# Moving a seven-for-eight block product from the second to the first product of each MLP layer

## The chip, the cores and the metric

The kernel runs on one core of one Trainium2 chip. The metric is device time in microseconds (us); one execution is also recorded by the hardware profiler, and all rows below come from that record. TensorE (PE) multiplies and loads its weights (PEld) from on-chip memory (SBUF) and writes only to its accumulators (PSUM, 8 banks of 512 fp32 values per partition). VectorE (DVE) and ScalarE (ACT) read and write both, GpSimd (POOL) works on SBUF, and SP issues the transfers between the chip's main memory and SBUF.

## The reference, cut to what matters

```python
X = np.fft.rfft(x, axis=1)                        # x: 2 x 3008 x 256
y = np.fft.irfft(X * (filt_r + 1j * filt_i), n=3008, axis=1).reshape(6016, 256)
g = y @ w_gate                                    # 256 -> 1536
y = (g / (1 + np.exp(-g)) * (y @ w_val)) @ w_out  # 1536 -> 256
h = y @ w_in                                      # 256 -> 2048
out = (h * np.clip(h + 3, 0, 6) / 6) @ w_out2     # 2048 -> 256
```

The two layers are called layer 1 and layer 2 below, and in each of them the first product goes from 256 to the wide side and the second product comes back.

## The kernel before

**Precision.** Both products must be better than one pass of TensorE gives. Each operand is split into a high part (a cast to the matmul type, on ACT) and a low part (the rest, a subtraction), and each product is made of three matmuls: low weight times high data, high weight times high data, high weight times low data. The helper `split` and the methods `high` and `low` are these splits.

**Stages.** First comes the Fourier stage (`over_n1`, `over_n2`, `filter_product`, `back`), which reads x and the filters and writes the spectrum to the buffers `d2` in main memory. `to_time` turns a part of it into one block of activations. A block has 512 tokens (448 for the last of each of the two batches), and there are 12 blocks. Then come layer 1 for all blocks and layer 2 for all blocks. Layer 1 writes its results to `yd`, layer 2 reads them back (`load_y`, `split_y`).

**The weights** arrive as 64-bit words. `Decode` makes fp32 of them in six steps (`part`, on DVE, the last one mostly on POOL). While layer 1 works on the first two blocks, which alternate, its weights are decoded one hidden chunk of 128 at a time and split into `wall`, where they stay until layer 1 ends. Layer 2's output weights are decoded during layer 1, put aside in `wd`, and brought back and split on ACT and POOL at the end of layer 1; its input weights are split into `wi2`.

**The two products.** One step takes a pair of hidden chunks and one block. `l1` is the plain first product: 12 matmuls of 512 columns per chunk in layer 1 (gate and value), 6 in layer 2. `l2` is the second product in the scheme of seven block products for eight (two chunks by two output halves by two token halves): 7 products of 3 matmuls are 21 matmuls of 256 columns. Its operands are sums: `Hidden.differences`, `rest`, `high` and `low` form the sums of the activations on DVE and split them, `weight_sums` forms those of the weights, and `gather` adds the seven products up at the end of a block. For the first two blocks of layer 1 the second product is plain (`l2_plain`, 12 matmuls of 512 columns per pair).

**What sets the order.** The program is written out by hand; each engine works through its instructions in that order and waits for semaphores. PSUM is divided into four banks `gv` for first products and four banks `a` for second products. In layer 1 the second product of a pair follows one pair later, in layer 2 two pairs later, so that its operands have a pair's time or more to be formed.

The excerpt below shows the lines that the change touches: `l1` is line 232, `l2` line 244, `l2_plain` line 254, `minus` and `plus` are lines 110 and 113 (all subtractions and additions on DVE and POOL are recorded under these two), `split` is line 117, the activation and product of layer 1 are lines 626 and 635, those of layer 2 lines 772 and 773.

Of the kernel before, what the change touches and what calls it, by code (L numbers as in the profile page):

```python
# [16 lines left out]
P = 128  # L17
# [29 lines left out]
def _token_times(time):  # L47

    order = []
    for j, n in BLOCKS:  # L50
# [28 lines left out]
def fft_conv_glu_mlp(ctx: ExitStack, tc: tile.TileContext, x, filt, mats, sgn, w1, w2, out):  # L79
# [44 lines left out]
    def new_g():  # L124
        return work.tile([P, 7 * D], F32, tag="g", name="g", bufs=1)

    def turns(j, n):

        return 32 * j // N1, -(-(32 * j + n // 2) // N1)

    def load_g(b, j):
        t0, t1 = turns(*BLOCKS[j][:1], BLOCKS[j][1] * N2)
        g = new_g().rearrange("p (t c) -> p t c", c=D)
        for r in range(2):
            nc.sync.dma_start(out=g[rows(r, N1P), :t1 - t0],
                              in_=d2[b].rearrange("q (h n) c -> (q h) n c", h=2)[:, 32 * r + t0:32 * r + t1])
        return g[:, :, :P], g[:, :, P:]

    def new_xs():
        return work.tile([P, 2, 2, 512], F32R, tag="xs", name="xs")  # L140

    def to_time(g, j, tag="gv"):

        accs = [bank(tag), bank(tag)]
        first, n = BLOCKS[j][0], BLOCKS[j][1] * N2
        t0, t1 = turns(first, n)
        lo, hi = 32 * first, 32 * first + n // 2
        for a in range(2):
            for t in range(t0, t1):
                i0, i1 = max(lo, t * N1), min(hi, (t + 1) * N1)  # L150
                for o in range(0, P, 64):
                    for r in range(2):
                        nc.tensor.matmul(accs[r][o:o + 64, a * 256 + i0 - lo:a * 256 + i1 - lo],  # L153
                                         g[a][rows(r, N1P), t - t0, o:o + 64],
                                         mat[rows(r, N1P), FIN + i0 - t * N1:FIN + i1 - t * N1])
        return accs

    def time_halves(xs, accs, j, r):
        n = BLOCKS[j][1] * 32
        src = accs[r].rearrange("p (a n) -> p a n", a=2)[:, :, :n]  # L160
        return xs[:, 0, :, r * n:(r + 1) * n], xs[:, 1, :, r * n:(r + 1) * n], src
# [55 lines left out]
    PAIRS = ((0, 0), (1, 2), (4, 5), (5, 4), (2, 6), (3, 3), (6, 1))  # L217
    PLACE = ((0, 0), (0, 1), (1, 0), (1, 1), (2, 0), (2, 1), (3, 0))
    WHERE = dict(zip(("P1", "P2", "P6", "P7", "P4", "P5", "P3"), PLACE))

    blocks = [(b, j) for b in range(B) for j in range(NB)]
    n_block = len(blocks)

    def ntok(k):
        return BLOCKS[blocks[k][1]][1] * N2

    def l1(acc, w, xs, n, part=(0, 1, 2)):

        for i in part:
            r, v = ((0, 0), (0, 1), (1, 0))[i]  # L230
            for k in range(2):
                nc.tensor.matmul(acc[:, :n], w[:, r, k * P:(k + 1) * P], xs[:, v, k, :n],  # L232
                                 start=(r, v, k) == (0, 0, 0), stop=(r, k) == (1, 1))

    def l2(acc, w, hidden, first, last):
        hs, nt = hidden.hs, hidden.nt

        terms = list(zip(PAIRS, PLACE))
        if last:
            terms.sort(key=lambda term: term[0][1] > 2)  # L240
        for v, ws in ((0, (1, 0)), (1, (0,))):
            for (iw, ih), (b, h) in terms:
                for r in ws:
                    nc.tensor.matmul(acc[b][:, 256 * h:256 * h + nt], w[:, r, iw], hs[:, v, ih, :nt],  # L244
                                     start=first and h == 0 and v == 0 and r == 1,
                                     stop=last and v == 1 and (h == 1 or b == 3))

    def l2_plain(acc, w, hidden, first, last):
        hs = hidden.hs
        for v, ws in ((0, (1, 0)), (1, (0,))):  # L250
            for j in range(2):
                for i in range(2):
                    for r in ws:
                        nc.tensor.matmul(acc[j], w[:, r, ((0, 1), (3, 2))[j][i]], hs[:, v, 2 * i:2 * i + 2],  # L254
                                         start=first and (v, i, r) == (0, 0, 1), stop=last and (v, i) == (1, 1))
# [8 lines left out]
    class Hidden:  # L264


        def __init__(self, nt):
            self.nt = nt
            self.h = mlp.tile([P, 8, 256], F32, tag="h", name="h")

        def chunk(self, i):
            return self.h[:, 2 * i:2 * i + 2, :self.nt]

        def halves(self, bank):
            return bank[:, :2 * self.nt].rearrange("p (t n) -> p t n", t=2)

        def values(self, a, b):
            return self.h[:, a:b, :self.nt]

        def parts(self, r, a, b):  # L280
            return self.hs[:, r, a:b, :self.nt]

        def begin(self, pool):

            self.differences(pool)
            self.rest()

        def differences(self, pool):

            self.hs = pool.tile([P, 2, 7, 256], F32R, tag="hs", name="hs", bufs=2 if pool is mlp else 1)  # L290
            v = self.values
            nc.scalar.copy(out=self.parts(0, 0, 3), in_=v(1, 4))  # L292
            minus(v(4, 6), v(1, 3), v(0, 1).to_broadcast([P, 2, self.nt]))

        def rest(self):

            v = self.values
            plus(v(6, 7), v(5, 6), v(1, 2))
            minus(v(7, 8), v(6, 7), v(3, 4))
            minus(self.parts(1, 0, 3), v(1, 4), self.parts(0, 0, 3).bitcast(F32))  # L300

        def high(self):
            nc.scalar.copy(out=self.parts(0, 3, 7), in_=self.values(4, 8))  # L303

        def low(self):
            minus(self.parts(1, 3, 7), self.values(4, 8), self.parts(0, 3, 7).bitcast(F32))

        def plain(self, pool):

            self.hs = pool.tile([P, 2, 7, 256], F32R, tag="hs", name="hs", bufs=2)  # L310
            split(self.parts(0, 0, 4), self.parts(1, 0, 4), self.values(0, 4))

    def new_y():
        return work.tile([P, 1024], F32, tag="y", name="y", bufs=1)

    def gather(acc, nt, scale, last=None):

        y = new_y()[:, :4 * nt]
        q = y.rearrange("p (j t n) -> p j t n", j=2, t=2)
        at = {name: acc[b][:, 256 * h:256 * h + nt] for name, (b, h) in WHERE.items()}  # L320

        def step(o, name, other):
            if scale == 1.0:
                plus(o, other, at[name])
            else:
                nc.vector.scalar_tensor_tensor(out=o, in0=at[name], scalar=scale, in1=other,
                                               op0=ALU.mult, op1=ALU.add)

        c00, c01, c10, c11 = q[:, 0, 1], q[:, 0, 0], q[:, 1, 1], q[:, 1, 0]
        nc.scalar.mul(out=c01, in_=at["P1"], mul=scale)  # L330
        p45 = work.tile([P, 2, 256], F32, tag="sm", name="p45", bufs=1)[:, :, :nt]
        nc.scalar.mul(out=p45, in_=acc[2].rearrange("p (h n) -> p h n", h=2)[:, :, :nt], mul=scale)
        step(c10, "P6", c01)
        step(c00, "P2", c01)
        step(c11, "P7", c10)
        step(c01, "P3", c10)
        minus(c10, c11, p45[:, 0])
        both = y.rearrange("p (j t) -> p j t", j=2)
        if last:
            for j, engine in ((1, nc.sync), (0, nc.scalar)):  # L340
                minus(q[:, j, 0], q[:, j, 0], p45[:, 1])
                engine.dma_start(out=last[j], in_=both[:, j])
            return
        minus(q[:, :, 0], q[:, :, 0], p45[:, 1:2].to_broadcast([P, 2, nt]))
        return both
# [497 lines left out]
```

## Time and profile before

| | us |
|---|---|
| median of 3 runs (1168.34 to 1170.76) | 1169.61 |
| the profiled execution, its own time | 1174.74 |
| its span, first to last instruction | 1172.9 |
| PE busy in the span | 1156.9 |
| DVE busy | 1009.5 |
| ACT busy | 610.6 |
| POOL busy | 145.5 |

The profiled execution took 5.13 us more than the median, and its span is 1.84 us shorter than its own time. The profile is read from the top down. The busy times say which engine is full; the 40 slices say whether it is full throughout; the waits of that engine say how long it stood and for whom; the chain of waits, which goes back from the last instruction, says which pieces of work follow one another without a gap. The Fourier stage ends at about 79 us, the alternating first two blocks at about 189 us, layer 1 at about 665 us.

### The profile page before, as it was taken

The numbers are of one execution on the slowest core, as the hardware profiler recorded it, in microseconds if no ns is written. First come the engines' busy times: TensorE is split into PE (matmuls) and PEld (weight loads), VectorE is DVE, ScalarE is ACT, GpSimd is POOL, SyncE is SP. The second block draws the span as 40 slices with busy tenths as digits, with TensorE's granted clock in tenths as the row PEclk, the third lists the DMA queues.
The fourth block names the chain that finished last, engine by engine and source line by source line (L and its number), as shares of the span: only waits on it lengthen the run. The fifth ranks groups of instructions, "written<-read, shape, count | busy, mean of one in ns | idle before, by whom it ended". The sixth has DMA issues, their size and how long they took to land.

```text
span 1172.9 us, 21793 instructions
## 1 busy us (share of the span) xinstructions
PE 1156.9 (99%) x9036; PEld 1024.6 (87%) x9036; DVE 1009.5 (86%) x1575; ACT 610.6 (52%) x928; POOL 145.5 (12%) x152
## 2 busy tenths in 40 slices
PE   9989999999999999999999999999999999999997
PEld 7668888888899888888889988999999999899997
DVE  5879967776678888778888899999999999999997
ACT  5555434343434444444445555656666566666654
POOL 4643210000002222012122300000000000000000
PEclk9999999999999999999999999999999999999999
DMA  8873401110013230312103111011001101100100
GB/s 297 271 194 106 142 14 44 25 36 18 22 57 86 84 109 24 98 46 72 53 3 106 57 35 36 1 37 36 30 6 37 34 1 37 37 21 17 35 18 18
DMA packets 43301, 70.33 MB, mean 60 GB/s; under 512 B 3712, under 2 KB 25088, under 8 KB 43200
## 3 DMA queue, kind: packets, MB, share of 16 engines
q1 hardware_dynamic: 42512, 68.17, 19.1%
q8 instruction: 71, 1.16, 0.4%
q10 hardware_dynamic: 688, 0.75, 0.2%
q14 instruction: 30, 0.25, 0.1%
HBM read 46.62 MB, written 22.28 MB: 59 GB/s over the span
## 4 chain that ended last, share of the span: by engine, by line
PE 91%; DVE 4%; DMA 2%; issue 1%; ACT 1%; SPq 1%; POOL 0%; ACTq 0%; DVEq 0%
PE gv L232 52%; PE a L244 31%; PE a L254 3%; DVE hs L110 1%; PE gv L463 1%; PE gv L153 1%; PE a L437 1%; DMA xin<-x_in 1%; PE gv L421 1%; DVE h L773 1%; DVE h L110 1%; SPq L472 1%; ACT h L772 0%; DMA d<-turned 0%; DVE h L113 0%
## 5 line engine op out<-in xcount | busy, mean ns | idle before, releaser
L244 PEld LDWEIGHTS a<-hs,wall 128*128 128x128 f32 x3276 | 408.7, 191 | 12.9 <-ACT hs L303 1.0
L244 PE MATMUL a<-hs,wall 128*128 128x256 f32 (+1 forms) x3276 | 414.6, 282 | 1.3 <-issue 0.5
L232 PE MATMUL gv<-xs,wall 128*128 128x512 f32 (+1 forms) x1728 | 398.9, 386 | 0.0
L232 PEld LDWEIGHTS gv<-xs,wall 128*128 128x128 f32 x1728 | 320.9, 188 | 58.7 <-issue 1.2
L110 DVE TENSOR_TENSOR hs<-h,hs 128x768 fp32r<-128x768 f32 (+2 forms) x324 | 348.0, 1074 | 6.3 <-ACT hs L117 3.4
L232 PE MATMUL gv<-xs,wi 128*128 128x512 f32 (+1 forms) x1152 | 274.5, 387 | 0.0
L232 PEld LDWEIGHTS gv<-xs,wi 128*128 128x128 f32 x1152 | 210.2, 188 | 35.7
L303 ACT CAST hs<-h 128x1024 fp32r<-128x1024 f32 (+1 forms) x156 | 160.8, 1031 | 128.0 <-DVE h L110 127.9
L110 DVE TENSOR_TENSOR h<-h 128x512 f32<-128x512 f32 (+3 forms) x312 | 186.4, 597 | 6.7
L292 ACT CAST hs<-h 128x768 fp32r<-128x768 f32 (+1 forms) x156 | 128.1, 821 | 101.5 <-DVE h L635 69.5
L635 DVE TENSOR_TENSOR h<-h,gv 128x512 f32<-128x512 f32 (+1 forms) x144 | 96.8, 672 | 71.9 <-PE gv L232 65.0
L626 ACT ACTIVATE h<-gv 128x512 f32<-128x512 f32 (+1 forms) x144 | 84.8, 589 | 136.1 <-PE gv L232 135.2
L773 DVE SCALAR_TENSOR_TENSOR h<-h,gv 128x512 f32<-128x512 f32 (+1 forms) x192 | 128.9, 671 | 14.2 <-ACT h L772 8.0
L772 ACT ACTIVATE h<-gv 128x512 f32<-128x512 f32 (+1 forms) x192 | 108.6, 589 | 59.0 <-PE gv L232 39.4
L113 DVE TENSOR_TENSOR h<-h 128x256 f32<-128x256 f32 (+1 forms) x156 | 65.7, 421 | 2.1
L113 POOL TENSOR_TENSOR ww<-ww,wa 128x512 f32<-128x512 f32 x16 | 20.7, 1296 | 371.2 <-issue 191.6
L254 PE MATMUL a<-hs,wall 128*128 128x512 f32 x144 | 34.6, 389 | 0.0
L254 PEld LDWEIGHTS a<-hs,wall 128*128 128x128 f32 x144 | 27.0, 188 | 5.6
L110 POOL TENSOR_TENSOR wall<-x,wall 128x512 fp32r<-128x512 f32 (+1 forms) x20 | 23.9, 1217 | 59.4 <-ACT wall L492 59.4
L463 PE MATMUL gv<-us,mat 64*64 64x384 f32 x256 | 29.6, 522 | 1.4 <-issue 0.9
L110 POOL TENSOR_TENSOR us<-us 128x192 f32<-128x192 f32 x32 | 25.9, 808 | 28.3 <-DVE us L450 27.4
L428 ACT COPY first<-gv 128x384 f32<-128x384 f32 x30 | 14.5, 482 | 28.2 <-PE gv L421 28.2
(79 smaller groups left out, 622.6 us busy)
## 6 DMA issues: line engine op xcount, KB each, us to landing
raw<-w_in SPq DMA_DIRECT2D x16, 512.0 KB, 4.4
xin<-x_in SPq DMA_DIRECT2D x30, 256.0 KB, 5.2
x<-w_in SPq DMA_DIRECT2D x9, 768.0 KB, 4.7
d<-turned SPq DMA_DIRECT2D x32, 192.0 KB, 5.0
yd<-y SPq DMA_DIRECT2D x10, 512.0 KB, 2.9
g<-yd SPq DMA_DIRECT2D x10, 512.0 KB, 3.7
y_out<-y SPq DMA_DIRECT2D x20, 256.0 KB, 2.4
wt<-wd SPq DMA_DIRECT2D x8, 448.0 KB, 3.2
```

The lines of the kernel that those rows point to most:

```text
L110: (engine or nc.vector).tensor_tensor(out=out, in0=a, in1=b, op=ALU.subtract)
L113: (engine or nc.vector).tensor_tensor(out=out, in0=a, in1=b, op=ALU.add)
L232: nc.tensor.matmul(acc[:, :n], w[:, r, k * P:(k + 1) * P], xs[:, v, k, :n], start=(r, v, k) == (0, 0, 0), stop=(r, k) == (1, 1))
L244: nc.tensor.matmul(acc[b][:, 256 * h:256 * h + nt], w[:, r, iw], hs[:, v, ih, :nt], start=first and h == 0 and v == 0 and r == 1, stop=las ...
L254: nc.tensor.matmul(acc[j], w[:, r, ((0, 1), (3, 2))[j][i]], hs[:, v, 2 * i:2 * i + 2], start=first and (v, i, r) == (0, 0, 1), stop=last a ...
L292: nc.scalar.copy(out=self.parts(0, 0, 3), in_=v(1, 4))
L303: nc.scalar.copy(out=self.parts(0, 3, 7), in_=self.values(4, 8))
L463: nc.tensor.matmul(accs[r][rows(h), :2 * COLS].rearrange("p (o n) -> p o n", o=2), mat[rows(r), w:w + N2], u[rows(r), :, part], start=m == ...
L626: nc.scalar.activation(out=h, in_=hid[p].halves(gate), func=AF.Silu)
L635: nc.vector.tensor_tensor(out=h, in0=h, in1=hid[p].halves(val), op=ALU.mult)
L772: nc.scalar.activation(out=h, in_=pre, func=AF.Relu, bias=3.0)
L773: nc.vector.scalar_tensor_tensor(out=h, in0=h, scalar=6.0, in1=pre, op0=ALU.min, op1=ALU.mult)
```

## The change

Blocks are now 1,024 tokens (960 for the last of each batch), six in all. The first block is still done as two blocks of 512 with plain products while layer 1's weights are decoded. From then on the work is a list of 108 **units**: 60 of layer 1 (five blocks by 12 chunks) and 48 of layer 2 (six blocks by 8 pairs of chunks).

- The first product of a unit is the scheme of seven products for eight (token halves by two halves of the 256 inputs by gate and value, or by the two chunks of a pair). Each of the seven, named `00`, `01`, `11`, `S1` to `S4` after its weights, is 3 matmuls over half a block (512 or 480 columns). Its sums are formed in PSUM: ACT copies bank b1 into bank b2, TensorE adds further products to both, and DVE adds b2 to an SBUF copy (`s7`), once into bank b3 and once into SBUF (`v1`).
- The second product is plain: 12 matmuls in layer 1 and 24 in layer 2, issued by `fill` in pieces between the seven products of the next unit.
- `Hidden`, `l2` and `gather` go. The sums of the activations are formed once per block instead (`differ`, `x_high`, `x_low`: 4 subtractions, 7 casts, 7 subtractions).
- Weights don't stay split. They are kept in main memory as fp32 together with their sums (`w1f`, `w2f`); each unit's weights are fetched (`ask_unit`) and split on ACT and POOL (`split_unit`), again for every block.
- Work beside the units (decoding layer 2's weights, forming their sums, preparing the next block) is placed at four **spots** in each unit, A, B, C and T. `turn_x`, at spot T of two units per block in layer 1, runs `to_time` into two of the four `gv` banks and empties them. `take` empties the banks `a` of a finished block in the first unit of the next one, half on DVE and half on ACT.

```diff
         def low_w1(f, engine=None):
...
+            nc.sync.dma_start(out=w1f[f][:, :6 * P], in_=w)
...
+        def split_unit(s, engine=nc.gpsimd):
...
+                split(form[:, 0], form[:, 1], src[:, wide:wide + 7 * P], engine)
+                split(wo[:, 0], wo[:, 1], src[:, :wide], engine)
...
+        def product(acc, s, a, i, start):
+            k = units[s][0]
+            n, w = half(k), wu[s][0]
+            for q, (r, v) in enumerate(((0, 0), (0, 1), (1, 0))):
+                nc.tensor.matmul(acc[:, :n], w[:, r, FORM[a] * P:(FORM[a] + 1) * P], xs_part(k, v, i),
+                                 start=start and q == 0, stop=q == 2, skip_group_check=True)
...
+        for g in range(G2):
             for i in range(2):
...
+                s = F1 * (1 + g // 2) + 3 * (g % 2) + i
+                add(s - 1, "C", ask_w2, g, i)
+                add(s, "A", lambda g, i: dec2[g, i].start(), g, i)
+                add(s, "B", lambda g, i: (dec2[g, i].part(0), dec2[g, i].part(1)), g, i)
+                add(s, "C", lambda g, i: dec2[g, i].part(2), g, i)
+                add(s + 1, "A", lambda g, i: (dec2[g, i].part(3), dec2[g, i].part(4)), g, i)
+                add(s + 1, "B", lambda g, i: dec2[g, i].part(5), g, i)
+                add(s + 1, "C", keep_w2, g, i)
...
+            product(b1, s, "00", 0, True)
+            if prev.kind:
+                prev.act(1, 0, pending[:, :prev.n])
+            product(b3, s, "S3", 5, True)
+            nc.scalar.copy(out=b2[:, :n], in_=b1[:, :n])
+            if prev.kind:
+                prev.times(1, 0, prev.v1 if prev.kind == 1 else pending[:, :prev.n])
+            fill()
+            nc.scalar.copy(out=u.s7, in_=b3[:, :n])
+            if prev.kind == 2:
+                prev.act(1, 1, prev.v1)
+                prev.times(1, 1, prev.v1)
+            if prev.kind:
+                prev.high(1)
+            spot(s, "A")
+            product(b2, s, "S2", 4, False)
+            plus(b3[:, :n], b2[:, :n], u.s7)
+            product(b1, s, "01", 1, False)
+            u.act(0, 0, b1[:, :n])
+            split_unit(s + 2)
+            if prev.kind:
+                prev.low(1)
+            fill()
+            if f == 0:
+                take(prev, 0)
+            spot(s, "B")
+            product(b2, s, "S1", 3, False)
+            if kind == 2:
+                u.times(0, 0, b1[:, :n])
+            plus(u.v1, b2[:, :n], u.s7)
+            product(b3, s, "11", 6, False)
+            if kind == 2:
+                u.act(0, 1, b3[:, :n])
+            u.times(0, kind - 1, b3[:, :n])
+            fill()
+            u.high(0)
+            free, role = pending, [b1, b3, b2]
+            spot(s, "T")
+            product(b2, s, "S4", 2, False)
+            spot(s, "C")
+            u.low(0)
+            fill()
```

On TensorE in the middle of layer 1 the order before alternates whole first products (`L232`: gate and value of one chunk into two `gv` banks, then those of the other chunk) with whole second products (`L244`, into four banks `a`).

```order
L232 MATMUL gv_3316<-xs_2963,wall_74 128x512 x6
L232 MATMUL gv_3317<-xs_2963,wall_74 128x512 x6
L232 MATMUL gv_3340<-xs_2963,wall_74 128x512 x6
L232 MATMUL gv_3341<-xs_2963,wall_74 128x512 x6
L244 MATMUL a_3288<-hs_3330,wall_74 128x256 x4
L244 MATMUL a_3289<-hs_3330,wall_74 128x256 x4
L244 MATMUL a_3290<-hs_3330,wall_74 128x256 x4
L244 MATMUL a_3291<-hs_3330,wall_74 128x256 x2
L244 MATMUL a_3288<-hs_3330,wall_74 128x256 x2
L244 MATMUL a_3289<-hs_3330,wall_74 128x256 x2
L244 MATMUL a_3290<-hs_3330,wall_74 128x256 x2
```

One unit of layer 1 after the change, with `L645` the seven products (into the banks gv0 to gv3, here b1 = gv2, b3 = gv3, b2 = gv0) and `L690` the pieces of the second product of the unit before:

```order
L645 MATMUL gv2_109<-xs_4372,wu_5355 128x512 x3
L645 MATMUL gv3_110<-xs_4372,wu_5355 128x512 x3
L690 MATMUL a0_111<-hs_5389,wo_5252 128x512 x2
L690 MATMUL a2_113<-hs_5389,wo_5252 128x512 x2
L645 MATMUL gv0_107<-xs_4372,wu_5355 128x512 x3
L645 MATMUL gv2_109<-xs_4372,wu_5355 128x512 x3
L690 MATMUL a0_111<-hs_5389,wo_5252 128x512
L690 MATMUL a2_113<-hs_5389,wo_5252 128x512
L690 MATMUL a1_112<-hs_5389,wo_5252 128x512 x2
L645 MATMUL gv0_107<-xs_4372,wu_5355 128x512 x3
L645 MATMUL gv3_110<-xs_4372,wu_5355 128x512 x3
```

All matmuls are now 512 columns wide (or 480), a unit's seven products return to the same three banks within the unit, and between two uses of bank gv0 stand 7 matmuls (the 3 of `01` or `11` and the 4 of `fill`).

On VectorE before, where a word of layer 2's weights is decoded (`ww`, `wa`) in layer 1: the product with the gate, the sums of the activations and their low parts follow.

```order
L193 TENSOR_SCALAR ww_3784<-wa_3757 128x512
L196 SCALAR_TENSOR_TENSOR ww_3784<-raw_3714,ww_3784 128x512
L199 TENSOR_SCALAR wa_3757<-ww_3784 128x512
L201 SCALAR_TENSOR_TENSOR wa_3757<-raw_3714,wa_3757 128x512
L635 TENSOR_TENSOR h_3759<-h_3759,gv_3794 128x2x224
L110 TENSOR_TENSOR h_3759<-h_3759 128x2x224
L113 TENSOR_TENSOR h_3759<-h_3759 128x224
```

One unit of layer 1 after, in which the same work stands at the spots (A: two rows ahead of the first addition `L119`, B: two rows ahead of the second, C: one row behind the product):

```order
L672 TENSOR_TENSOR h_4082<-h_4082 128x512
L200 TENSOR_SCALAR wa_4098<-ww_4119 128x512
L202 SCALAR_TENSOR_TENSOR wa_4098<-raw_4076,wa_4098 128x512
L119 TENSOR_TENSOR gv1_108<-gv2_109,h_4145 128x512
L116 TENSOR_TENSOR hs_4081<-h_4082,hs_4081 128x512
L192 TENSOR_SCALAR wa_4163<-wa_4163 128x512
L194 TENSOR_SCALAR ww_4185<-wa_4163 128x512
L119 TENSOR_TENSOR h_4145<-gv2_109,h_4145 128x512
L672 TENSOR_TENSOR h_4145<-h_4145,gv1_108 128x512
L197 SCALAR_TENSOR_TENSOR ww_4185<-raw_4139,ww_4185 128x512
L116 TENSOR_TENSOR hs_4144<-h_4145,hs_4144 128x512
```

The two additions `L119`, for which TensorE's next product into b2 waits, now stand behind the decoding steps of spots A and B in VectorE's row.

On POOL before, the last work is seven splits of a weight pair (`wt`) at the end of layer 1, and layer 2 has none:

```order
L110 TENSOR_TENSOR wi2_5177<-ww_6447,wi2_5177 128x2x256
L110 TENSOR_TENSOR wall_74<-wt_6774,wall_74 128x896
L110 TENSOR_TENSOR wall_74<-wt_6801,wall_74 128x896
L110 TENSOR_TENSOR wall_74<-wt_6874,wall_74 128x896
L110 TENSOR_TENSOR wall_74<-wt_6940,wall_74 128x896
L836 UNCONDITIONAL_BRANCH
```

After, POOL splits a unit's weights (`wu` and `wo` from the fetched `st`) in every unit to the end:

```order
L116 TENSOR_TENSOR wu_9659<-st_9555,wu_9659 128x896
L116 TENSOR_TENSOR wo_9660<-st_9555,wo_9660 128x512
L116 TENSOR_TENSOR wu_9729<-st_9627,wu_9729 128x896
L116 TENSOR_TENSOR wo_9730<-st_9627,wo_9730 128x512
L934 UNCONDITIONAL_BRANCH
```

There are 108 such pairs of rows (`wo` is 256 wide in the 60 units of layer 1).

## Rows read from the trace of the kernel before

**Rows 1.** The page: busy us, share and instructions; TensorE's granted clock in tenths.

```profile
PE 1156.9 (99%) x9036; PEld 1024.6 (87%) x9036; DVE 1009.5 (86%) x1575; ACT 610.6 (52%) x928; POOL 145.5 (12%) x152
...
PEclk9999999999999999999999999999999999999999
```

**Rows 2.** Waits of PE: for whom, us in total, times, longest.

```profile
PE gv L421 <- issue: 3.4, 3, 1.7
PE a L153 <- DMA g<-d: 2.3, 2, 1.8
```

**Rows 3.** Chain of waits, first two blocks: start us, us, what.

```profile
135.78 5.44 PE gv L232 x24
141.22 2.72 PE a L254 x12
```

**Rows 4.** The same chain, blocks of 512 in layer 1 and in layer 2.

```profile
317.04 2.51 PE a L244 x21
319.55 5.47 PE gv L232 x24
...
926.09 2.51 PE a L244 x21
928.61 2.75 PE gv L232 x12
```

**Rows 5.** The same chain, blocks of 448 in layer 1.

```profile
334.91 4.87 PE gv L232 x24
339.78 2.34 PE a L244 x21
```

**Rows 6.** The same chain, blocks of 448 in layer 2.

```profile
1147.50 2.43 PE gv L232 x12
1149.93 2.33 PE a L244 x21
```

**Rows 7.** Timeline, layer 2: start us, us, engine, operation, [idle before <-releaser].

```profile
1036.39 2.67 PE L244 MATMUL a<-hs,wall 128*128 128x256 f32 x21
1036.59 0.60 ACT L772 ACTIVATE h<-gv 128x512 f32<-128x512 f32 x1 [0.31 <-PE gv L232]
```

**Rows 8.** Groups by shape: busy us, mean ns of one | idle before them.

```profile
L773 DVE SCALAR_TENSOR_TENSOR h<-h,gv 128x512 f32<-128x512 f32 x160 | 109.2, 682 | 11.5 <-ACT h L772 6.2
...
L117 ACT CAST wall<-wt 128x896 fp32r<-128x896 f32 x8 | 7.5, 937 | 1.4 <-DMA wt<-wd 1.4
...
L193 DVE TENSOR_SCALAR ww<-wa 128x512 uint32<-128x512 uint32 x16 | 6.8, 427 | 1.3
```

**Rows 9.** Timeline of POOL and DVE, end of layer 1.

```profile
630.99 0.62 DVE L110 TENSOR_TENSOR h<-h 128x448 f32<-128x448 f32 x1
...
641.01 2.12 POOL L110 TENSOR_TENSOR wall<-wt,wall 128x896 fp32r<-128x896 f32 x1 [2.58 <-ACT wall L117]
...
641.55 2.07 DVE L110 TENSOR_TENSOR h<-h 128x448 f32<-128x448 f32 x1
...
646.56 5.10 POOL L110 TENSOR_TENSOR wall<-wt,wall 128x896 fp32r<-128x896 f32 x2 [3.42 <-ACT wall L117]
...
649.58 0.61 DVE L635 TENSOR_TENSOR h<-h,gv 128x448 f32<-128x448 f32 x1
```

**Rows 10.** Stretch 0 to 60 us: busy us of engines, PEclk, DMA share, GB/s.

```profile
0.00:60.00 60.00, 54.97 (x1318) 42.39 (x1322) 41.22 (x72) 31.36 (x85) 34.59 (x56) 0.97 0.89 284
```

**Rows 11.** Chain of waits, end of the Fourier stage and end of the kernel.

```profile
56.03 7.00 DMA xin<-x_in
...
1165.00 1.39 PE a L244 x10
...
1169.01 0.30 DVEq L836
```

**Rows 12.** One line by form: the matmuls of `to_time`.

```profile
L153 PEld LDWEIGHTS gv<-mat,g 48*64 48x64 f32 x992 | 15.4, 135 | 3.5 <-issue 3.5
```

More of the change, by code (lines that the diff above doesn't have):

```diff
@@ L49, in _token_times @@
     order = []
-    for j, n in BLOCKS:
+    for j, n in WIDE:
         n = n * N2 // 2
@@ L231, in l1, with l2_plain @@
             for k in range(2):
-                nc.tensor.matmul(acc[:, :n], w[:, r, k * P:(k + 1) * P], xs[:, v, k, :n],
+                nc.tensor.matmul(acc, w[:, r, c[k]:c[k] + P], xs[:, v, k],
                                  start=(r, v, k) == (0, 0, 0), stop=(r, k) == (1, 1))
[L235 to L249, printed above, removed]
+    def l2_plain(k, p, hs, first, last):
         for v, ws in ((0, (1, 0)), (1, (0,))):
@@ L262, in weight_sums @@
         minus(sm[:, 3], a01, sm[:, 1], engine)
[L264 to L311, printed above, removed]
@@ L313, in new_y @@
-    def new_y():
[L314 to L345, printed above, removed]
@@ new lines, in add, with spot, evacuate, quarter @@
+        def add(s, spot, step, *a):
+            jobs.setdefault((s, spot), []).append(lambda: step(*a))
+        def spot(s, name):
+            for step in jobs.pop((s, name), ()):
+                step()
+        def evacuate(k, accs, a):
+            n = half(k)
+            nc.scalar.copy(out=xr[k][:, ORDER.index(2 * a), :n], in_=accs[0][:, :n])
+            nc.vector.tensor_copy(out=xr[k][:, ORDER.index(2 * a + 1), :n], in_=accs[1][:, :n])
+        def quarter(k, i):
+            return xr[k][:, i, :half(k)]
@@ L632, in fft_conv_glu_mlp @@
                 dec[f_].start()
-            if i == 0 and p > plain:
-                hid[p - 1].high()
-            nc.vector.tensor_tensor(out=h, in0=h, in1=hid[p].halves(val), op=ALU.mult)
-            if i == 0 and p > plain:
-                hid[p - 1].low()
+            nc.vector.tensor_tensor(out=h, in0=h, in1=val, op=ALU.mult)
             if t == 0:
@@ new lines, in fft_conv_glu_mlp, with ask_x, turn_x @@
+        ys, gx = {}, {}
+        def ask_x(k, stage):
+            if stage == 1:
+                gx[k] = load_g(*blocks[k][:2], 2 * half(k))
+            else:
+                xr[k] = new_raw()
+                nc.sync.dma_start(out=xr[k][:, 0:4, :half(k)], in_=yd[k][:, :, :half(k)])
+        def turn_x(k, a):
+            accs = (free, role[0])
+            to_time(gx[k][a], blocks[k][1], 2 * half(k), accs, a)
+            if a == 0:
+                xr[k] = new_raw()
+                begin_x(k)
+            evacuate(k, accs, a)
@@ L799 @@
+        u, b2 = prev, role[2]
+        second = list(u.second())
+        u.act(1, 0, b2[:, :n])
+        u.times(1, 0, b2[:, :n])
+        u.act(1, 1, u.v1)
+        u.times(1, 1, u.v1)
+        for step in second[:12]:
+            step()
+        u.high(1)
+        take(u, 0)
+        u.low(1)
+        for step in second[12:]:
+            step()
+        take(u, 1)
 def kernel(**inputs):
```

545 lines of the change are left out of this document (301 added, 244 removed).

## The prediction

> **What bounds the kernel now.** I read the busy times first, then TensorE's waits, then the chain of waits, then the durations by shape, and last the timeline where GpSimd works. TensorE is busy for 1156.9 of 1172.9 us and holds a granted clock in the top tenth throughout [rows 1]. Its waits are few and all in the Fourier stage [rows 2]: the longest kinds sum to 3.4 and 2.3 us. So nothing but TensorE's own work sets the time of the two layers, and VectorE, though 86% busy, never stops it there. The chain shows the pace. In the first two blocks, where all matmuls are 512 wide, 24 take 5.44 us and 12 take 2.72 [rows 3]: 0.2267 us each. In layer 1 a pair is 5.47 + 2.51 = 7.98 us, in layer 2 2.75 + 2.51 = 5.26 [rows 4]; for blocks of 448 tokens 4.87 + 2.34 = 7.21 [rows 5] and 2.43 + 2.33 = 4.76 [rows 6]. A matmul of 256 columns thus takes 2.51/21 = 0.1195 us, more than half of one of 512: by the two rows each matmul costs about 0.0124 us whatever its width.
>
> The kernel to be compared is the profiled execution, 1174.74 us: a span of 1172.9 and 1.84 around it. The median is 1169.61, 5.13 less; I sum against the first and take 5.13 off.
>
> **Matmuls: -43 us.** Outside the Fourier stage and the first two blocks TensorE spends 8 blocks x 6 pairs x 7.98 + 2 x 6 x 7.21 in layer 1 and 10 x 8 x 5.26 + 2 x 8 x 4.76 in layer 2, which is 383.0 + 86.5 + 420.8 + 76.2 = 966.5 us. A unit has 21 matmuls in its seven products and 12 or 24 in its plain second product: 33 in layer 1, 45 in layer 2. With 3 blocks of 512-wide and 2 of 480-wide units in layer 1 and 4 and 2 in layer 2, that is 36 x 33 + 32 x 45 = 2628 of 512 columns and 24 x 33 + 16 x 45 = 1512 of 480. At 0.2267 (and 0.2147 for 480, midway between it and 4.87/24 = 0.2029) they take 595.8 + 324.6 = 920 us, 46 less. At the pace of layer 2's first products, 2.75/12 = 0.2292 (and 0.2160), they take 929, 38 less. I take 43 and keep both. In columns alone the change is worth little, 2.1%: layer 2's pairs have the same 23,040 columns per 1,024 tokens as before. The rest comes from fewer, wider matmuls.
>
> The Trainium skill ("TensorE: Matmul & The Clock Gate", section "Back-to-back issue gap") puts the spacing of warm matmuls at N/2.4 + 2.5 ns, which is 216 ns for 512 columns and 109 for 256. By it the two kernels would need about 896 and 873 us, a gain of 23. The trace has 226.7 and 119.5, a larger fixed part.
>
> **Smaller terms.** `to_time` issues 40 program matmuls fewer in the two layers (456 for 496), each recorded as two passes of 15.4/992 = 0.0155 us [rows 12]: -1.2. At the end, TensorE's last 10 matmuls begin at 1165.00 and take 1.39; the span ends 6.5 us later, because the seven products must still be added up and the output is issued only at 1169.01 [rows 11]. The new end is one copy and the output, but the last unit's activations come first. I take -1 (0 to -2). In front, the first 60 us move 284 GB/s with the transfer engines 89% busy, and a load of x that lands at 63 us is on the chain [rows 10, 11]. The change puts one more store of 128 x 768 fp32, 393 KB, ahead of the last loads of x on SP's queue: 393 KB at 284 GB/s is +1.4 (0 to +3, as SP also waits there for VectorE's low part, with two steps of loads of x and the stores of `d2` queued behind it).
>
> **The new chains inside a unit.** Before, a second product's operands had a pair's time to form. Now TensorE waits within a unit for ACT (copy of b1 into b2) and for VectorE (two additions that read b2). I lay a layer 1 unit out from rows: 3 matmuls 0.68 us, 4 fills 0.91; ACT starts 0.2 us after TensorE went on to the next group [rows 7]; ACT passes of 512 columns 0.60 [rows 7], VectorE passes on 512 columns 0.68 [rows 8]. From the unit's start the products end thus: `00` 0.68, `S3` 1.36, `S2` 2.95, `01` 3.63, `S1` 5.21, `11` 5.89, `S4` 7.48. ACT's copy is done at 0.68 + 0.2 + 0.6 = 1.48, `S2` starts at 2.27: 0.8 to spare. The first addition is done at 2.95 + 0.2 + 0.68 = 3.83, `S1` starts at 4.53: 0.7 to spare. The second is done at 6.09, `S4` starts at 6.80: 0.7 again. In layer 2 the fills are 6, and the same sums leave 1.2, 1.2 and 1.0. A bare unit therefore costs nothing more. That addition and copy write PSUM, which no row of before shows; I take the nearest rows, and 0.7 us of cover stands for their error.
>
> **POOL now holds VectorE in every unit.** At the end of layer 1 a subtraction with both inputs in SBUF, which takes 0.62 us alone, took 2.07 when it met POOL's split of 896 columns (641.01 to 643.13): it ended 0.49 after POOL did. A product that reads PSUM ran in 0.61 in the middle of such splits [rows 9]. So VectorE's SBUF-only passes wait for the whole of a POOL pass, and what is queued behind them waits too, PSUM or not. POOL goes from 7 such splits to 108. In a layer 1 unit, ACT casts at 4.43 to 5.37 (0.94 [rows 8]) and POOL splits from 5.4 to 7.5. In a bare unit only VectorE's last subtraction (`low(0)`) meets it, and nobody needs that before 3.6 of the next unit: hidden.
>
> **Units with more work on VectorE: +30 us (0 to +76).** Here the queue ahead of the two additions grows.
> - Decoding: 16 half-words, each with two passes of 0.43 [rows 8] at spot B, behind `low(1)` (to 4.5): done at 5.4, just when POOL begins. In the two units at a block's start, `take` (I put it at ACT's 0.60) stands in front as well; the second pass then falls behind POOL, ends at about 8.0, and the addition at 8.7 for 6.8: 1.9 us. 4 blocks x 2 units x 1.9 = 15.
> - Preparing the next block: two subtractions of 0.68 at A move the first addition from 3.83 towards 4.6 to 5.1 for 4.53. About 0.8 per block in layer 1, 5 blocks: 4. In layer 2 one more of 0.68 at B stands ahead of the second addition, 0.5 to 0.6 late in two units, with the 0.15 at A about 1.6 per block, 5 blocks: 8.
> - `to_time`'s two banks are emptied by ACT and VectorE (0.6) while only `S4` (0.68) runs: 0.4 x 8 = 3.
>
> Upper end: each of the 36 units with VectorE work at spot B (16 decoding, 10 and 10 preparing) is held by one POOL pass of 2.12: 76. I take 30, since the layout above hits the pass in some of them only.
>
> **The seam: +4 (0 to +8).** In the last three steps of the first two blocks VectorE gets 11 more passes of 0.68 (7.5 us) in about 11 us of TensorE time, while POOL splits two units and forms sums. What hides it is VectorE's free time there; if POOL takes that, the first unit starts late.
>
> **Sum.** -43 - 1.2 - 1 + 1.4 + 30 + 4 = -9.8: 1164.9 for a profiled execution, 1160 against the median, 0.8% faster.
>
> **The rivals.**
> 1. *All extra work stays in the shadow.* For it: TensorE waits for nobody now, with VectorE 86% busy [rows 1, 2]. Against: it had a pair's time of slack, and now 0.7 us. Extras 5, seam 2: 1169.6 - 43 - 1.2 - 1 + 1.4 + 7 = 1133. Chance 0.22.
> 2. *Slower: VectorE is caught behind POOL's 896-column pass ahead of the second addition.* Price 2.1 us a time. It decides from (43 + 2.2 - 1.4 - 4)/2.1 = 19 catches, net of other losses; at all 36, 1169.6 - 39.8 + 76 = 1206; at 28, where I place it, 1189. For it: the pass in rows 9 and a margin of 0.7. Against: PSUM readers are not held. Chance 0.26.
> 3. *Weights come late.* For chunks 4 to 11 of layer 1 the sums are formed on POOL, stored, and fetched again within two units; ACT's split, ahead of `high(0)`, would wait. My layout has the fetch land about when ACT asks, with 2 us of cover; 8 units x 2 late would be +16: 1176. Chance 0.05.
> 4. *The pace goes by columns alone*, and the wide matmuls give back nothing: 966.5 x 2.1% = 20 us of gain in place of 43: 1183. Rows 3 and 4 speak against it. Chance 0.03. The rule of the Trainium skill cited above comes nearest to it, with 23.
>
> My forecast has the rest, 0.44.
>
> **The numbers.** A change of 0.2% (2.3 us) is about what a measurement of this kernel tells from none. Faster than 1167.3: most of the forecast's spread and rival 1, 0.64. Slower than 1171.9: rivals 2 to 4 and a little of the forecast, 0.29. Between: 0.07. Range: from near rival 1, 1131, to rival 2's middle, 1189.
>
> **What will show it.** Pieces of plain matmuls at 12 in 2.72 confirm the first term. TensorE's waits on VectorE's addition (now line 119) should sum to some 20 to 30 us, at the first units of a block and in the three units that prepare one, and on ACT's copy to little; POOL's pass of 896 beside a stretched VectorE pass marks each. I am wrong if bare units show waits (a PSUM-writing copy or addition that is far slower), if the waits are nearly nil, or if TensorE's clock falls.

## The result and the profile after

The changed kernel takes 1185.59 us (median of four runs, 1185.27 to 1186.2) against 1169.62 (1168.34 to 1170.76): ratio 1.0137, 95% interval 1.012 to 1.0155. It is 1.4% slower; the forecast was 1160, 0.8% faster. The profiled execution has a span of 1183.7 us, 10.8 more than before.

TensorE has less to do and stands more. The page of the kernel after, for the first line of [rows 1]:

```profile
PE 1135.6 (96%) x7232; PEld 931.3 (79%) x7232; DVE 879.9 (74%) x1164; ACT 741.6 (63%) x1255; POOL 493.4 (42%) x391
```

Busy time fell from 1156.9 to 1135.6 us, and what TensorE did not work rose from 16.0 to 48.1 us. Where this is shows in two stretches of either trace, layer 1 and layer 2 (columns: stretch, its length; busy time of PE, PEld, DVE, ACT, POOL; granted clock, DMA share, GB/s). Before:

```profile
178.40:664.40 486.00, 485.94 (x3573) 432.24 (x3572) 388.07 (x596) 215.95 (x317) 75.83 (x63) 1.00 0.19 56
664.40:1172.90 508.50, 501.31 (x3191) 457.73 (x3189) 484.32 (x779) 308.58 (x434) 0.20 (x1) 1.00 0.08 25
```

After:

```profile
178.10:690.90 512.80, 475.81 (x2704) 387.92 (x2703) 384.35 (x517) 314.56 (x559) 251.58 (x201) 0.97 0.42 131
690.90:1183.70 492.80, 488.58 (x2175) 405.89 (x2173) 354.60 (x456) 340.45 (x528) 164.42 (x94) 1.00 0.27 91
```

Layer 2 is 15.7 us shorter, and no wait of TensorE is listed in it. Layer 1 is 26.8 longer: 37 us idle, and a mean clock of 0.97. With -0.3 ahead of both that makes the 10.8.

The pace of units that nothing disturbs is in the timeline of PE (start, duration, engine, line, tiles, count). The nine matmuls that close one unit and open the next recur every 7.48 to 7.50 us with 512 columns and every 7.15 with 480; a unit of layer 2 takes 10.20:

```profile
190.23 2.20 PE L645 MATMUL gv<-xs,wu 128*128 128x512 f32 x9
197.73 2.20 PE L645 MATMUL gv<-xs,wu 128*128 128x512 f32 x9
205.21 2.20 PE L645 MATMUL gv<-xs,wu 128*128 128x512 f32 x9
...
361.54 2.11 PE L645 MATMUL gv<-xs,wu 128*128 128x480 f32 x9
368.68 2.11 PE L645 MATMUL gv<-xs,wu 128*128 128x480 f32 x9
...
981.05 0.84 PE L645 MATMUL gv<-xs,wu 128*128 128x512 f32 x3
991.25 0.84 PE L645 MATMUL gv<-xs,wu 128*128 128x512 f32 x3
```

So 60 undisturbed units of layer 1 would take 36 x 7.48 + 24 x 7.15 = 441 us. They took 512.8, from 178.1 to the first unit of layer 2 at 690.9. From the starts of all units in the timeline the other 72 divide thus: 14 are `to_time` in eight units (its 96 matmuls take 1.5 us each time, and before it was there as well), 5 are the seam, 5 one stall in the fourth unit, and 47 lie in the six units of each block of layer 1 from the second on in which layer 2's weights are decoded (units 12 to 17, 24 to 29, 36 to 41, 48 to 53). The waits of PE, for [rows 2]:

```profile
PE gv L645 <- DVE h L119: 22.6, 10, 4.7
PE a L690 <- ACT hs L678: 6.0, 4, 3.6
PE gv L645 <- DVE gv L119: 5.0, 9, 1.6
```

VectorE's addition L119 is named, 27.6 us in all, as forecast. But the releaser is only the last link. The longest of these waits, 4.66 us in unit 15, in the timelines of SP, POOL, ACT, DVE and PE:

```profile
310.37 0.59 ACT L678 CAST hs<-h 128x480 fp32r<-128x480 f32 x1 [0.35 <-DVE h L672]
311.58 0.96 POOL L116 TENSOR_TENSOR sm<-ww,sm 128x128 f32<-128x128 f32 x1
312.57 0.32 SPq L790 DMA_DIRECT2D w2f<-sm  x1
312.98 0.38 SPq L178 DMA_DIRECT2D raw<-w_in  x1
317.02 0.66 ACT L183 ACTIVATE wa<-raw 128x512 f32<-128x512 f32 x1 [6.06 <-DMA raw<-w_in]
317.72 0.43 DVE L192 TENSOR_SCALAR wa<-wa 128x512 f32<-128x512 f32 x1 [5.50 <-ACT wa L183]
318.52 0.65 DVE L119 TENSOR_TENSOR h<-gv,h 128x480 f32<-128x480 f32 x1
319.23 3.97 PE L645 MATMUL gv<-xs,wu 128*128 128x480 f32 x9 [4.66 <-DVE h L119]
```

POOL does nothing between 312.5 and 319: it holds nobody. SP's queue stands at `w2f<-sm`, the store of the weight sums, until POOL has formed them at 312.5; behind it waits the request for the next raw words. They land at 317, ACT has stood 6.06 us for them with everything it owes to the unit queued behind, VectorE 5.50 for ACT, TensorE 4.66 for VectorE. Waits of this kind are there four times, in units 15, 27, 39 and 51 (4.66, 4.10, 4.15, 3.19 us). After each TensorE is slow for a while. Nine matmuls take 3.97 in place of 2.11, at a granted clock of 0.50, the lower of the two levels:

```profile
319.20:323.00 3.80, 3.77 (x10) 3.15 (x11) 3.80 (x4) 1.78 (x4) 3.08 (x2) 0.50 0.00 1
323.00:325.50 2.50, 2.50 (x11) 2.16 (x10) 1.75 (x4) 1.62 (x3) 0.00 (x0) 0.85 0.75 236
```

That is 1.9 us more for the nine and 0.4 for the four behind them.

The wait of 3.60 us in the fourth unit is of the same family, one step longer:

```profile
186.75 0.42 SPq L516 DMA_DIRECT2D wq<-w1f  x1
198.58 0.90 POOL L119 TENSOR_TENSOR sm<-wq 128x128 f32<-128x128 f32 x1 [8.63 <-DMA wq<-w1f]
201.21 0.34 SPq L513 DMA_DIRECT2D w1f<-sm  x1
203.24 0.32 SPq L497 DMA_DIRECT2D st<-w1f  x1
209.20 0.94 ACT L123 CAST wu<-st 128x896 fp32r<-128x896 f32 x1 [6.37 <-DMA st<-w1f]
211.02 1.99 PE L690 MATMUL a<-hs,wo 128*128 128x512 f32 x4 [3.60 <-ACT hs L678]
```

The fetch for chunk 4's sums, issued just behind the load of the next block's spectrum (`g<-d`), lands 11.8 us later; POOL forms the sums, SP stores them, and only then asks for the unit's weights.

What the prediction described is there too, but small. In the first unit of a block (unit 12; 24, 36 and 48 alike):

```profile
287.27 2.11 POOL L116 TENSOR_TENSOR wu<-st,wu 128x896 fp32r<-128x896 f32 x1 [4.51 <-ACT wu L123]
287.43 2.22 DVE L194 TENSOR_SCALAR ww<-wa 128x512 uint32<-128x512 uint32 x1
289.58 0.65 DVE L119 TENSOR_TENSOR h<-gv,h 128x480 f32<-128x480 f32 x1
290.28 2.22 PE L645 MATMUL gv<-xs,wu 128*128 128x480 f32 x9 [1.41 <-DVE h L119]
```

A pass of 0.43 us takes 2.22 beside POOL's, the addition comes late, and TensorE stands 1.41.

### The profile page after: what moved, and what is told of

It is laid out like the page before. It is cut to its first block, busy times and chain, and to the rows that moved or that the text cites. A ratio compares the mean times of both kernels' runs of the same rounds, so it can differ in the third digit from the quotient of the medians.

```text
span 1183.7 us, 18655 instructions
## 1 busy us (share of the span) xinstructions
PE 1135.6 (96%) x7232; PEld 931.3 (79%) x7232; DVE 879.9 (74%) x1164; ACT 741.6 (63%) x1255; POOL 493.4 (42%) x391
## 5 line engine op out<-in xcount | busy, mean ns | idle before, releaser
L645 PE MATMUL gv<-xs,wu 128*128 128x512 f32 (+1 forms) x2268 | 582.1, 393 | 30.6 <-DVE h L119 22.6
L645 PEld LDWEIGHTS gv<-xs,wu 128*128 128x128 f32 x2268 | 426.9, 191 | 126.4 <-DVE h L119 30.4
L690 PE MATMUL a<-hs,wo 128*128 128x512 f32 (+1 forms) x1872 | 482.7, 388 | 6.4 <-ACT hs L678 6.0
L116 POOL TENSOR_TENSOR wu<-st,wu 128x896 fp32r<-128x896 f32 x108 | 234.7, 2173 | 555.1 <-ACT wu L123 522.4
L690 PEld LDWEIGHTS a<-hs,wo 128*128 128x128 f32 x1872 | 352.9, 189 | 77.4 <-ACT hs L678 9.9
L116 DVE TENSOR_TENSOR hs<-h,hs 128x1024 fp32r<-128x1024 f32 (+3 forms) x228 | 238.8, 1047 | 71.8 <-ACT hs L678 68.1
L678 ACT CAST hs<-h 128x512 fp32r<-128x512 f32 (+3 forms) x216 | 172.6, 799 | 168.5 <-DVE h L672 95.3
L116 POOL TENSOR_TENSOR wo<-st,wo 128x256 fp32r<-128x256 f32 (+1 forms) x108 | 124.5, 1153 | 0.0
L123 ACT CAST wu<-st 128x896 fp32r<-128x896 f32 x108 | 100.8, 934 | 6.4 <-DMA st<-w1f 6.4
L119 DVE TENSOR_TENSOR gv<-gv,h 128x512 f32<-128x512 f32 (+1 forms) x108 | 73.9, 684 | 41.0 <-PE gv L645 32.9
L668 ACT ACTIVATE h<-gv 128x512 f32<-128x512 f32 (+1 forms) x144 | 84.0, 583 | 19.4 <-PE gv L645 18.5
L119 DVE TENSOR_TENSOR h<-gv,h 128x512 f32<-128x512 f32 (+1 forms) x108 | 73.0, 676 | 28.5 <-PE gv L645 28.2
```

The costliest lines, as they stand in the source:

```text
L116: (engine or nc.vector).tensor_tensor(out=out, in0=a, in1=b, op=ALU.subtract)
L119: (engine or nc.vector).tensor_tensor(out=out, in0=a, in1=b, op=ALU.add)
L123: nc.scalar.copy(out=hi, in_=src)
L645: nc.tensor.matmul(acc[:, :n], w[:, r, FORM[a] * P:(FORM[a] + 1) * P], xs_part(k, v, i), start=start and q == 0, stop=q == 2, skip_group_c ...
L668: nc.scalar.activation(out=self.value(t, a), in_=src, func=AF.Relu, bias=3.0)
L678: nc.scalar.copy(out=self.hs[:, t, :, 0, :self.n], in_=self.value(t))
```

## Experiments

Two theories: **P**, the prediction's (POOL's pass of 896 columns holds VectorE's passes ahead of the second addition), and **L** (transfers come too late, because they stand on SP's queue behind stores that wait for POOL or behind a large load). Each kernel is the changed one with the edit shown; ratios are to the kernel before on the same chip.

**Raw words asked for earlier** (`e1_raw_early`).

```diff
-                add(s - 1, "C", ask_w2, g, i)
+                add(s - 1, "A", ask_w2, g, i)
```

> The changed kernel, with one line moved: the raw words of each decoded half (ask_w2) are asked for at spot A of the unit ahead instead of spot C, so that on SP's queue they stand ahead of the store of the weight sums, which waits for POOL. Theory L (late transfers): in the fourth unit of four of layer 1's blocks ACT stood about 6 us for these words, and TensorE 4.7, 4.1, 4.2 and 3.2 us behind it, with about 2 us more each at half the granted clock afterwards. These 24 us go: 1162 (1158 to 1168). Theory P (the prediction's: POOL's pass of 896 columns holds VectorE ahead of the second addition): the long waits have nothing to do with the ask, 1184 to 1187.

Measured 1162.31 (1158.35 to 1163.16), ratio 0.9918 (0.9892 to 0.9943): L, and one line turns the change from 1.4% slower to 0.8% faster. The request is now out at 302.70, ACT takes the words without a wait, and unit 15 takes 7.15 (306.31 to 313.46):

```profile
302.70 0.45 SPq L178 DMA_DIRECT2D raw<-w_in  x1
306.31 2.11 PE L645 MATMUL gv<-xs,wu 128*128 128x480 f32 x9
308.93 0.32 SPq L786 DMA_DIRECT2D w2f<-ww  x1
309.95 0.67 ACT L183 ACTIVATE wa<-raw 128x512 f32<-128x512 f32 x1
313.46 2.12 PE L645 MATMUL gv<-xs,wu 128*128 128x480 f32 x9
```

**Sums' fetches ahead of the spectrum** (`e2_sums_first`). The lines that register `form_wq` and `form_sums` stand ahead of the calls of `plan_x`.

> The changed kernel, with the fetches for the sums of layer 1's chunks 4 and 5 (form_wq) put ahead of the load of the next block's spectrum (ask_x) in the first unit. Theory L: the 3.6 us that TensorE stands in the fourth unit at 207 us come from a chain fetch, sums on POOL, store, ask for the unit's weights; the fetch took 11.8 us behind the spectrum's load. The wait and 1.8 us at half clock behind it go: 1180 (1179 to 1182). If the transfers are slow by themselves there, whatever their order, the wait stays: 1185. If the spectrum, now asked later, comes late for to_time in the seventh unit: 1186 or more.

Measured 1179.35 (1177.88 to 1182.69), ratio 1.0078 (1.0049 to 1.0107). The fourth unit takes 7.48 in place of 12.97: L again.

**Two passes moved behind the addition** (`e3_parts_at_C`).

```diff
-                add(s, "B", lambda g, i: (dec2[g, i].part(0), dec2[g, i].part(1)), g, i)
-                add(s, "C", lambda g, i: dec2[g, i].part(2), g, i)
+                add(s, "C", lambda g, i: dec2[g, i].leading(), g, i)
```

> The changed kernel, with VectorE's first two passes of each decoded half taken from spot B (ahead of the second addition) to spot C (behind it). Theory P: these two passes, caught behind POOL's pass, hold the addition in all 16 decoding units; nearly all of TensorE's 27.6 us on VectorE's additions go, and the half clock behind them: 1153 (1150 to 1162). Theory L: only the wait at the four block starts (1.4 to 1.5 us each) is of that kind, the long ones stay: 1179 (1176 to 1182).

Measured 1184.54 (1183.72 to 1185.76), ratio 1.0115 (1.0095 to 1.0135). Neither number. The waits at the block starts went (unit 12 takes 7.30 for 8.88, unit 24 7.51 for 9.11), so they were what P says; the passes then met POOL's next work, and the low part behind them came late:

```profile
PE a L690 <- ACT hs L678: 12.9, 17, 3.8
PE gv L645 <- DVE gv L119: 8.1, 16, 1.6
PE a L690 <- DVE hs L116: 5.5, 5, 1.5
```

**POOL's pass in two halves** (`e4_pool_halves`).

```diff
-                split(form[:, 0], form[:, 1], src[:, wide:wide + 7 * P], engine)
+                nc.scalar.copy(out=form[:, 0], in_=src[:, wide:wide + 7 * P])
+                for c in (slice(0, 448), slice(448, 896)):
+                    minus(form[:, 1, c], src[:, wide:wide + 7 * P][:, c], form[:, 0, c].bitcast(F32), engine)
```

> The changed kernel, with POOL's pass of 896 columns in every unit's split cut into two of 448 (about 0.2 us more of POOL in each unit). If a POOL pass holds VectorE's passes for its whole length, a pass that meets it is let go after half the time: the four waits at block starts fall from 1.4 to about 0.4 us. Theory P, all the waits on additions being of that kind: 1170. Theory L: the long ones stay, 1181 (1178 to 1184). If the hold is not by passes (VectorE comes in only when POOL is idle): 1185 to 1189, with 0.2 us more per unit on POOL.

Measured 1184.31 (1182.03 to 1187.69), ratio 1.0115 (1.0088 to 1.0141). In unit 12 the hold is by passes: VectorE's pass is let go after 1.27, in the middle of POOL's pair, and the wait is 0.46 as expected. The gain is given back in the next unit (9.33 for 7.73), but not by POOL: the raw words asked for at 284.06, behind the spectrum's load, land 11.7 us later, ACT waits 3.14 for them, and TensorE goes on at 297.95, where it did at 298.01 in the changed kernel. ACT waits for raw words in units 25 and 37 as well (2.68 and 2.54). So the gain is lost to L. The rows of this run and, behind the dots, ACT's row of the changed kernel:

```profile
284.06 0.42 SPq L178 DMA_DIRECT2D raw<-w_in  x1
286.56 2.43 POOL L116 TENSOR_TENSOR wu<-st,wu 128x448 fp32r<-128x448 f32 x2 [3.84 <-ACT wu L507]
286.73 1.27 DVE L194 TENSOR_SCALAR ww<-wa 128x512 uint32<-128x512 uint32 x1
288.62 2.21 PE L647 MATMUL gv<-xs,wu 128*128 128x480 f32 x9 [0.46 <-DVE h L119]
295.74 0.66 ACT L183 ACTIVATE wa<-raw 128x512 f32<-128x512 f32 x1 [3.14 <-DMA raw<-w_in]
...
295.80 0.67 ACT L183 ACTIVATE wa<-raw 128x512 f32<-128x512 f32 x1 [1.89 <-DMA raw<-w_in]
```

**Both transfers** (`e5_early_and_first`).

> The changed kernel with both edits to the order of transfers (raw words at spot A of the unit ahead; the sums' fetches ahead of the spectrum's load). Theory L: the two stalls are separate, so the gains add, 23 and 6: 1156 (1154 to 1159). If one of them only moves when the other goes: 1160 or more.

Measured 1156.67 (1153.66 to 1157.4), ratio 0.9859 (0.9822 to 0.9895): the gains add. What is left in the decoding units, by their lengths in the timeline, is some 24 us. ACT still waits for raw words in units 13, 25 and 37 (1.11, 1.77 and 0.72), so a small part of the 24 may be L.

**The last decoding step off POOL** (`e6_no_pool_part`): `part(5)` with `nc.vector`.

> The same, and the last step of each half's decoding (part 5, 512 columns, 1.7 us on POOL) is done by VectorE, at its place at spot B. What is left after the transfers are some 24 us in the decoding units. Theory P2 (POOL's passes hold VectorE's passes on SBUF, here the product L672 of the next unit, which took 1.6 to 1.7 us beside that step): the waits on ACT's high part that follow it go, about 6 us: 1150 (1147 to 1153). If the length of VectorE's queue decides, 0.7 us more at spot B makes the second addition later: 1156 to 1160.

Measured 1159.38 (1157.31 to 1162.17), ratio 0.9889 (0.9856 to 0.9922): P2's number falls, and the other theory's (1156 to 1160) holds. The waits on ACT's high part went (2.8 us in the kernel before this one), but those on the second addition rose from 8.4 to 19.4:

```profile
PE gv L645 <- DVE h L119: 19.4, 13, 2.3
```

The 0.68 us more at spot B pushed the next pass into POOL's: in unit 16 `L194` starts 0.78 after POOL and takes 1.80. This points to the moment, whether VectorE's passes at B have started when POOL starts its 896 columns; the next runs test it.

**The decoding spread out** (`e7_spread`). Same passes, other spots, and the last step and the weight sums on VectorE in place of POOL. The spots, here for the three halves of a block that begin at units q = 1, 4 and 6 of it:

```diff
+                    plans[4 * b + h] = ((q - 2, "A"), (q - 1, "B"), (q, "A", 0, 1), (q, "B", 2), (q + 1, "A", 3, 4), (q + 1, "B", 5))
```

> The sums' fetches ahead, and the decoding of layer 2's weights spread over the units: the same passes, all of them and the sums now on VectorE, at most about 1.1 us at spot A and 0.7 to 0.9 at spot B of a unit, none at C, none at B of a block's first unit, and in the last block not in the units that prepare layer 2's first block; raw words two spots or more ahead. Theory P2 with L: a pass that ends before POOL's split begins, 5.4 us into a unit, costs TensorE nothing, so nearly all of the 24 us goes: 1133 (1129 to 1139). If VectorE's work as such is too much for these units, wherever it stands: 1148 or more, since VectorE has 9 us more to do than in the kernel before this one.

Measured 1142.09 (1141.54 to 1147.34), ratio 0.975 (0.9716 to 0.9785). 9 us above the expectation, and 6 below the 1148 of the other theory: the decoding units ran at 7.15 or 7.48 but for three (27, 39, 54), where four passes for the weight sums stand at B, and unit 28, which took 9.23 because the granted clock was 0.50 behind the stall of unit 27. This run changes spots and engines at once. The last run below puts the last step back on POOL; the weight sums were not put back, so their share is not shown.

**The seam** (`e8_spread_seam`): the casts and subtractions of the expectation registered at spots A and B of unit 0.

> The same, and at the seam two casts (ACT) and three subtractions (VectorE) of the first unit's activations go from the last plain step into the first unit. TensorE stood 1.7, 1.2 and 1.3 us there. If ACT's and VectorE's queues make these waits: 2 to 3 us less than the kernel before this one, 1130. If POOL's split of the second unit makes them (it holds VectorE's low parts): no change, 1133.

Measured 1140.65 (1138.97 to 1143.78), ratio 0.9731 (0.9698 to 0.9764). The intervals of the two overlap, so this edit is not settled. Its waits changed their names: 1.7, 1.2 and 1.3 became 1.1 on VectorE's product and 1.8 on low parts that POOL's split of the second unit holds. In the units 27, 39 and 54 TensorE stands 2.3 to 2.5 us each. Unit 27, DVE and POOL:

```profile
391.70 0.29 DVE L119 TENSOR_TENSOR sm<-ww 128x128 f32<-128x128 f32 x1 [0.71 <-DMA w2f<-sm]
391.81 2.15 POOL L116 TENSOR_TENSOR wu<-st,wu 128x896 fp32r<-128x896 f32 x1 [4.66 <-ACT wu L123]
392.02 2.08 DVE L116 TENSOR_TENSOR sm<-sm,ww 128x128 f32<-128x128 f32 x1
394.76 0.28 DVE L116 TENSOR_TENSOR sm<-ww,sm 128x128 f32<-128x128 f32 x1
394.96 0.68 DVE L119 TENSOR_TENSOR h<-gv,h 128x512 f32<-128x512 f32 x1
```

A pass of 128 columns, 0.28 us by itself, takes 2.08 when it starts 0.2 after POOL. (The first had waited 0.71 for the store that empties the same buffer.)

**The sums in two parts** (`e9_sums_split`): two passes at A of unit 24, 36 or 48, two at B of unit 27, 39 or 54, in a second buffer.

> The spread kernel with the seam's edit, and the three sums of weights that still stood as four passes at spot B (units 27, 39 and 54) as two passes at A of an earlier unit and two at B. There a first pass of 128 columns took 2.08 us beside POOL's pass and TensorE stood 2.2 to 2.5 us; two passes end before POOL begins. If the place decides: 3 x 2.4 = 7 us less than the kernel with the seam's edit, 1133 (1131 to 1136). If the number of VectorE's passes in these units decides, wherever they stand: 1139 to 1142.

Measured 1133.52 (1130.25 to 1135.88), ratio 0.9664 (0.9639 to 0.9689): 3.4% faster than the kernel before, the fastest here. In unit 27 the last pass now starts 0.2 before POOL and is not held (0.29), and TensorE waits for no decoding anywhere:

```profile
396.42 0.29 DVE L116 TENSOR_TENSOR sm<-ww,sm 128x128 f32<-128x128 f32 x1
396.63 2.13 POOL L116 TENSOR_TENSOR wu<-st,wu 128x896 fp32r<-128x896 f32 x1 [4.66 <-ACT wu L123]
396.73 0.69 DVE L119 TENSOR_TENSOR h<-gv,h 128x512 f32<-128x512 f32 x1
```

Layer 1 takes 459.6 us for the 512.8 of the changed kernel, TensorE busy in 456.5 of them, at full clock:

```profile
181.80:641.40 459.60, 456.54 (x2705) 381.26 (x2704) 372.00 (x565) 315.21 (x559) 203.51 (x153) 1.00 0.45 146
```

The edit does two things, it moves two passes and takes away the wait of 0.71 for the buffer; which of them counts more is not shown.

**The last step back on POOL** (`e10_part_on_pool`), nothing else changed.

> The kernel before this one with one thing put back: the last step of each half's decoding runs on POOL again (1.7 us, 16 times), at the same place in the program. Theory P2 (a POOL pass holds what VectorE needs next): it follows POOL's splits, reaches into the next unit and holds VectorE's product there, 0.7 to 1.6 us a unit as in the kernel with the raw words early: 11 to 25 us more, 1144 to 1158. If only VectorE's queue ahead of the additions counts: the same or a little faster, 1130 to 1134.

Measured 1134.96 (1133.84 to 1136.0), ratio 0.9682 (0.9654 to 0.971): not to be told from the kernel before it. The lengths of the units, which leave out what varies ahead of them, show more: layer 1's 60 units take 462.0 us for 458.2, most of it in units 54 (8.68 for 7.15) and 59 (8.15 for 7.15). So with the rest in place POOL's extra pass costs some 4 us, far from the 11 to 25 of P2; who does the step matters less than when VectorE's passes run.

## Why the prediction was wrong

**Matmuls, -43: right.** 36 x 7.48 + 24 x 7.15 + 32 x 10.20 + 16 x 9.75 = 923.3 against 966.5 before: -43.2. The two price bounds were 920 and 929. Rival 4 (columns alone) falls with it. The Trainium skill ("TensorE: Matmul & The Clock Gate", section "Back-to-back issue gap") calls N/2.4 + 2.5 ns the gap of an isolated matmul, 216 ns for 512 columns, and gives about 131 as measured in a stream. Neither is the price here: 10.20/45 is 226.7 ns.

**Bare units, 0: right.** The layout gave `S2`'s bank 0.7 to 0.8 us to spare, and no undisturbed unit waits; the copy and the addition that write PSUM take 0.55 to 0.57 and 0.66 to 0.70, close to the 0.60 and 0.68 taken from the rows of before. **`to_time`, -1.2:** the row in [rows 12] is that of its weight loads; the matmuls take 1.54/96 = 0.016 us each, so the term holds.

**Front, +1.4: not settled.** The first plain matmul came at 77.05, before the change at 78.70. But in the last three kernels above, alike up to there, the first unit begins at 177.02, 181.84 and 177.03 us. **End, -1:** 4.2 us from the last matmul (1179.5) to the end of the span for 6.5 before, -2.3. **Seam, +4:** 1.74 + 1.19 + 1.30 = 4.2, right in size. `to_time`'s two banks: 1 to 2 for 3.

**Units with extra work, +30 (0 to +76): the step that failed**, in size and in mechanism. It was worth some 56: 47 in the decoding units, 5 in the fourth, 1 to 2 at `to_time`, and 3 in layer 2.
- I costed the decoding by VectorE's passes alone (15 us) and took its raw words as there when ACT asks. But the diff shows `keep_w2` and the next `ask_w2` at spot C of the same unit, in this order: SP's request stands behind a store that waits for four POOL passes. By e1 this was 23 us, half clock included. SP's queue was the one that I did not walk through. The Trainium skill says it in general ("DMA: Bandwidth & Descriptors", section "Anatomy of one DMA — SWDGE (gpsimd) path": a semaphore wait happens on the issuing sequencer before dispatch, not in the DMA engines); rows 312.57 and 312.98 above, where SP is the issuing queue, agree.
- For rival 3 (late weights) I had "2 us of cover" for the chain fetch, sums, store, ask. It was right once in place of eight times: 6 us by e2, because the first fetch was queued behind the spectrum's load.
- POOL holding VectorE was right as a mechanism (2.22 for 0.43, 1.27 with half passes, 2.08 for 0.28) and in which engine TensorE is seen to wait for. At block starts it cost 1.41 to 1.50 in one unit of four blocks, where I had 1.9 in two of four. In the other decoding units it and its knock-on cost most of the rest, together with the block starts at most 23 by e5 and e9, where I had nothing.
- Preparing the next block, 4 + 8: next to nothing in layer 1's units 8 to 10, and in layer 2 0.4 to 0.65 us a block, 2.7 in all (units of 10.3 to 10.55 for 10.20), in pieces too short for the list of waits. It cost more only in layer 1's last block (units 48 to 53 lose 11.7 us in e5, those of the other blocks 3.5 to 4.7), where `x_low` and `differ` share three units with decoding, which the layout, made for one kind of extra work at a time, did not hold.
- TensorE's clock: I wrote that I'd be wrong if it fell, and gave that no price. It fell after the five long stalls and after one of 1.64 us in unit 50, at some 2 us each.

**The rivals.** Rival 2, slower by VectorE caught behind POOL, has the right sign and the right releaser's name, and TensorE's waits alone would have made it the whole cause. It is less than half of it: by e1 and e2 the late transfers are 23 + 6 us, by e5 and e9 the rest of the decoding at most 23. Rival 1 (all extra work hidden, 1133) is what the change gives once the requests and passes stand right: 1133.52. That the two agree to the last us is luck: the start of the first unit alone varies by 5 us.

## What to carry to other kernels

When a step is added, walk its instructions on every queue, SP's too: a request behind a store that waits for compute is late by that wait, and an in-order engine that asks for it passes the stall on to all. Follow a named releaser back until an engine is found that was late for a reason of its own. In a software pipeline with under 1 us to spare, the place of a 0.4 us pass against another engine's long pass can be worth more than who does it.

## What was not expected of the hardware

- After TensorE had stood 4.66 us its granted clock was 0.50, the lower level, and the next 13 matmuls cost 2.2 us more. All five stalls of 3.19 us and more in this kernel ended so. Shorter ones went either way: 1.64 us in unit 50 did (0.50 from 613.9 to 617.3), 1.64 in the same unit of `e1_raw_early` did not; 2.22 in unit 27 of `e7_spread` did, 2.25 in unit 27 of `e8_spread_seam` did not. After 1.41 us in unit 12 the next nine took 2.22, nearly the 2.11 of an undisturbed unit.
- Behind the spectrum's load (`g<-d`, two parts of 528 KB) a fetch of 384 KB landed 11.8 us after its issue, and one of 512 KB of raw words after 11.7; in the stretches around, the medians of the two kinds are 3.7 and 4.9.
